# Loading the query weights of a decode step in eight parts of sixteen partitions

## The chip, the cores and the metric

The kernel runs on one core of a Trainium2 chip. The metric is the device time of one execution in microseconds. Before the change it was 380.53 us, the median of three runs (380.45 to 380.88).

The core's engines are TensorE (PE in the profile; its weight loads are PEld), VectorE (DVE), ScalarE (ACT), GpSimd (POOL) and SyncE (SP). Sixteen DMA engines move data between memory and SBUF, the on-chip store of 128 partitions; here SyncE issues all large transfers, ScalarE four small ones.

## The reference

One token passes through an attention block with a cache of 65,536 positions, and through a gated MLP mixer; a gate g mixes the two. All inputs are bfloat16.

```python
# x [1,1,1024]; k_cache, v_cache [1,4,65536,128]; wq [1024,4096]; wo [4096,1024]
q = (x @ wq).reshape(1, 1, 32, 128).transpose(0, 2, 1, 3)
k, v = repeat(k_cache, 8, axis=1), repeat(v_cache, 8, axis=1)
p = softmax(einsum('bhqd,bhkd->bhqk', q, k) * 128 ** -0.5)
a = einsum('bhqk,bhkd->bhqd', p, v).transpose(0, 2, 1, 3).reshape(1, 1, 4096) @ wo

z = gelu(x @ w_in)                       # w_in [1024,3584]
z1, z2 = z[..., :1792], layernorm(z[..., 1792:])
b = (z1 * (w_sp * z2 + b_sp)) @ w_out    # one position: w_sp is one number

g = sigmoid((x * gate_w).sum(-1))
return g * a + (1 - g) * b
```

The caches hold 128 MiB (134 MB) of the 162 MB that the kernel reads.

## The kernel before

**An order written out by hand.** Every operation is recorded by `R.op` (called `P`) with its engine, the keys that it reads and the keys that it writes. A planner derives the semaphore waits from the keys, and each engine runs its operations in the order in which they were recorded. A transfer has a semaphore of its own, named by `dma=`, which counts sixteen when the transfer has landed. A key that was written by a transfer stands for that transfer.

**The stream of loads.** A list `stream` holds all large loads in the order in which they are issued: wq, then K steps 0 and 1 in one load of 8 MB (64 KB for each partition), w_in, K step 2, K step 3, w_out, then K and V in turn, and at the end five loads of wo. They share a ring in SBUF, one row of bytes for each partition. `issue()` sends the next load as soon as the operations that use the bytes under it have been recorded (`done`), and the load then waits on SyncE for these operations. SyncE's queue is in order: a load that waits holds back those behind it.

**The query weights.** wq has 1024 rows of 4096 columns. `rows(A_wq, 0, 8)` gives each of the 128 partitions eight consecutive rows, 65,536 bytes that lie in one piece in memory. `issue()` treats this load in a way of its own (`cut`): the last `MC = 512` columns of the eighth row are left out, so that a partition gets 64,512 bytes, and the missing 128 pieces of 1,024 bytes come through `few_rows()` (L398), right behind the load. That function issues eight small loads into another region of the ring, at `M_AT`: four with five partitions, four apart, of four pieces each, and four with three partitions and four pieces each. Index e of the load numbered `lo` goes to partition 4e + lo.

**Who uses them.** The group of matrix products that ends on L507 computes q. It is recorded as one operation on TensorE (L510), which waits for wq, for the eight small loads, for the transposed input `xT` and for `xe`. Behind it VectorE copies the result (L513), and the load of w_in goes out, since it takes wq's bytes in the ring. Then the K steps begin: VectorE transposes a quarter of a step (L548), TensorE multiplies it, four times for each step. Later, exponentials on ScalarE, V products, and the output products with wo follow; the last ones are at L766, then a copy (L827) and the store (L368).

**The start gate.** A program begins with a barrier between the engines. `emit` takes the first `R.ahead = 2 + MB = 10` instructions of SyncE (the wq load, the eight small loads, and the first K load) and puts them ahead of SyncE's part in this barrier, so that they are issued while the other engines wait for it. In the same way four small loads of ScalarE (`R.early`) go ahead of its part.

## Time and profile before

| what | value |
|---|---|
| median of three runs | 380.53 us |
| the profiled execution | 380.59 us |
| its span, first to last instruction | 379.3 us |
| TensorE busy, share of the span | 229.9 us, 61% |
| VectorE busy | 205.6 us, 54% |
| ScalarE busy | 23.3 us, 6% |
| GpSimd busy | 9.3 us, 2% |
| read from memory | 162.01 MB, 427 GB/s over the span |
| the wq load, 8064 KB, issue to landing | 21.7 us |
| the first K load, 35.4 us from issue, lands at | 42.1 us |
| TensorE begins the products with wq | 23.18 us |

The profile's page lists busy times by engine, the span in forty slices (digits are tenths of a slice; the row GB/s tells what all DMA engines moved in a slice of 9.5 us), the DMA queues, and the groups of instructions. A window's line gives its length, then the busy time and number of instructions for PE, PEld, DVE, ACT and POOL, the granted TensorE clock, the busy share of the DMA engines, and GB/s. In these windows a packet counts wholly where it starts, so the DMA share can be a little over 1. A line of the chain of waits gives the start in us, the length in us, and the line that ran or the transfer that was waited for. A line on a source line's instructions gives minimum, median and maximum of their durations in ns. In the SyncE timeline the columns are start, length, engine, line, and how many instructions.

### The profile page before, as it was taken

To read this page: it belongs to the slowest core of one execution; us is meant where nothing else is said; L and a number is where in the kernel's file an instruction comes from. 1 tells how busy PE (TensorE), PEld (TensorE's weight loads), DVE (VectorE), ACT (ScalarE), POOL (GpSimd) and SP (SyncE) were. 2 spreads that over 40 slices of the span, in tenths; PEclk is the share of its full clock that TensorE was granted. 3 is DMA by queue.
4 is the path that set the end of the run, shared out by engine and by line. 5 is a ranking of instruction groups with operands and counts; after the bars stand their busy time and mean duration, and the time that the engine had idled before them with its cause. 6 is when DMAs were issued, how large, how long until landed. Compare 5 with 4: busy or idle time off the path is not lost.

```text
span 379.3 us, 2599 instructions
## 1 busy us (share of the span) xinstructions
PE 229.9 (61%) x1452; PEld 57.9 (15%) x844; DVE 205.6 (54%) x168; ACT 23.3 (6%) x24; POOL 9.3 (2%) x36
## 2 busy tenths in 40 slices
PE   0062289566648934895389328951995189737296
PEld 0011011011201200121012001220111011201024
DVE  1411487778479625965496249745873387412020
ACT  1000000010420000002200000022000000220000
POOL 1400000000000000000000000000000000000000
PEclk9997589798959985998599959995899589958599
DMA  9999999999999999999999999999999999999896
GB/s 436 435 415 408 433 419 422 442 456 438 408 435 442 435 444 422 422 442 435 442 437 442 429 422 429 444 442 435 429 408 430 442 435 442 437 442 435 384 432 273
DMA packets 3822, 162.17 MB, mean 428 GB/s; under 512 B 484, under 2 KB 612, under 8 KB 868
## 3 DMA queue, kind: packets, MB, share of 16 engines
q1 hardware_dynamic: 3776, 162.01, 98.9%
q8 instruction: 9, 0.15, 0.1%
q10 hardware_dynamic: 36, 0.00, 0.0%
q14 instruction: 1, 0.01, 0.0%
HBM read 162.01 MB, written 0.00 MB: 427 GB/s over the span
## 4 chain that ended last, share of the span: by engine, by line
DMA 61%; PE 17%; DVE 17%; SPq 2%; ACT 1%; issue 1%
DMA arena<-in_A_k_cache_dram 46%; DVE arena L548 16%; DMA arena<-in_A_wo_dram 8%; DMA arena<-in_A_v_cache_dram 7%; PE scp L261 7%; PE scp L263 6%; SPq L409 2%; PE obt L261 2%; PE obt L263 1%; DVE arena L585 1%; PE fbt L766 1%; ACT arena L580 1%; DVE arena L670 0%; DVE arena L668 0%; PE fbt L714 0%
## 5 line engine op out<-in xcount | busy, mean ns | idle before, releaser
L548 DVE STREAM_TRANSPOSE arena<-arena 128x2048 f32<-128x2048 f32 x64 | 143.0, 2284 | 54.9 <-DMA arena<-in_A_k_cache_dram 40.1
L261 PE MATMUL scp<-arena 128*128 128x512 bf16 (+1 forms) x274 | 111.6, 424 | 94.4 <-DVE arena L548 93.9
L263 PE MATMUL scp<-arena 128*128 128x512 bf16 (+1 forms) x275 | 110.2, 418 | 0.0
L261 PE MATMUL obt<-arena 128*64 128x512 bf16 (+2 forms) x334 | 60.7, 404 | 15.1 <-DMA arena<-in_A_v_cache_dram 14.9
L263 PE MATMUL obt<-arena 128*64 128x512 bf16 (+2 forms) x333 | 60.1, 400 | 0.0
L261 PEld LDWEIGHTS scp<-arena 128*128 128x128 bf16 (+1 forms) x274 | 27.5, 104 | 205.1 <-issue 103.9
L585 DVE STREAM_TRANSPOSE arena<-arena 128x2048 bf16<-128x2048 bf16 x7 | 16.2, 2311 | 27.0 <-PE obt L263 24.8
L580 ACT ACTIVATE arena<-arena 128x2048 bf16<-128x2048 f32 x8 | 16.0, 2002 | 217.2 <-DVE arena L577 194.1
L261 PEld LDWEIGHTS obt<-arena 128*64 128x64 bf16 (+1 forms) x334 | 17.7, 109 | 65.3 <-issue 58.5
L565 DVE TENSOR_SCALAR_CACHE_REDUCE arena<-scp 128x2048 f32<-128x2048 f32 x8 | 18.3, 2292 | 16.0 <-PE scp L263 16.0
L614 DVE RECIPROCAL arena<-mbt 128x1 f32<-128x1 f32 x4 | 0.6, 138 | 17.5 <-PE mbt L609 17.5
L588 DVE STREAM_TRANSPOSE arena<-arena 128x1024 bf16<-128x1024 bf16 x2 | 2.5, 1245 | 12.9 <-PE obt L263 12.9
L536 POOL COPY arena<-arena 32x32 bf16<-32x32 bf16 x16 | 3.3, 204 | 227.4 <-PE scp L263 207.7
L467 PE MATMUL scp<-arena 8*128 8x1 bf16 x8 | 0.7, 198 | 13.0 <-DVE arena L462 13.0
L627 PE MATMUL mbt<-arena 128*64 128x128 bf16 x8 | 1.3, 314 | 7.7 <-DVE arena L621 7.7
L766 PE MATMUL fbt<-arena 128*32 128x128 bf16 x128 | 4.2, 220 | 1.2 <-DMA arena<-in_A_wo_dram 1.2
L280 DVE MEMSET mbt<- 128x512 f32 x1 | 0.5, 485 | 7.7 <-PEq L846 7.7
L513 DVE CAST arena<-obt 97x1024 bf16<-97x1024 f32 x1 | 1.2, 1224 | 6.2 <-PE obt L507 6.2
L475 PE MATMUL mbt<-arena 1*128 1x2 bf16 x1 | 0.2, 158 | 7.2 <-DMA arena<-in_B_b_sp_dram 7.2
L827 DVE CAST arena<-fbt 36x128 bf16<-36x128 f32 x1 | 0.3, 283 | 7.3 <-PE fbt L766 7.3
L477 DVE COPY arena<-mbt 128x2 f32<-128x2 f32 x1 | 0.2, 158 | 7.3 <-PE mbt L475 7.3
L577 DVE TENSOR_REDUCE arena<-mbt 128x1 f32<-128x32 f32 x4 | 0.8, 192 | 6.0 <-PE mbt L574 6.0
(99 smaller groups left out, 62.5 us busy)
## 6 DMA issues: line engine op xcount, KB each, us to landing
arena<-in_A_k_cache_dram SPq DMA_DIRECT2D x2, 4096.0 KB, 31.7
arena<-in_A_wq_dram SPq DMA_DIRECT2D x1, 8064.0 KB, 21.7
arena<-in_B_w_in_dram SPq DMA_DIRECT2D x1, 7168.0 KB, 28.9
arena<-in_A_wo_dram SPq DMA_DIRECT2D x1, 4096.0 KB, 38.5
arena<-in_B_w_out_dram SPq DMA_DIRECT2D x1, 3584.0 KB, 20.2
arena<-in_A_wo_dram SPq DMA_DIRECT2D x1, 2048.0 KB, 27.6
arena<-in_A_wo_dram SPq DMA_DIRECT2D x1, 1280.0 KB, 30.3
arena<-in_A_wo_dram SPq DMA_DIRECT2D x1, 512.0 KB, 31.0
```

Source lines behind the costliest of these rows:

```text
L261: return e.matmul(*a, **kw)
L263: one = e.matmul(*a, **kw).ins
L409: P("SP", lambda e, a=a, b=b: e.dma_start(a, b), w=[("few", lo + j0)] + ([] if lo + j0 else [("slot", x) for x in gr]), dma="few%d" % (lo ...
L513: P("DVE", lambda e: e.tensor_copy(psb[0:97, :], ob[0:97, :]), w=["psb", "ob"])
L536: P("POOL", lambda e, pb=pb: e.tensor_copy(vw(qpad, 24 + 32 * pb, [[QP, 4], [1, 8]], 32 * pb, 32), vw(qall, 8 * g, [[32, 4], [1, 8]], 32 * ...
L548: P("DVE", lambda e: e.transpose(ktb(i).bitcast(F32), sl[:, 4096 * p:4096 * (p + 1)].bitcast(F32)), r=keys[4 * p:4 * p + 4], w=[("kt", i % ...
L565: P("DVE", lambda e: e.tensor_scalar(scs(j), scp[:, :], 0.0, None, op0=ALU.add, op1=ALU.max, accum_out=maxc[:, j:j + 1]), w=[("sc", j % 2) ...
L580: P("ACT", lambda e: e.activation(psb2, scs(j), ACTF.Exp, bias=gcol(j // 2, K_NB), scale=SCALE, accum_out=lp[:, j:j + 1]), r=[("sc", j % 2 ...
L585: P("DVE", lambda e: e.transpose(ptsb2, psb2), r=["psb"], w=[("ptsb", 0), ("ptsb", 1)])
L588: P("DVE", lambda e: e.transpose(ptsb(n), ab("PSB", 1024, 1024 * (n % 2))), r=["psb"], w=[("ptsb", n % 2)])
L627: ins = e.matmul(mb[64 * g:64 * (g + 1), 0:128], vw(sel, 128 * c, [[2, 64]]), osc[:, 128 * c:128 * (c + 1)], start=(c == 0), stop=(c == 3) ...
L766: ins = e.matmul(fb[32 * b:32 * (b + 1), 0:QW], ovz[:, z:z + 32], sl[:, o:o + QW], start=False, stop=(i == 3 and c == 7), tile_position=(0 ...
```

## The change

For wq alone, the one load of 128 partitions becomes `NJ = 8` loads of sixteen partitions: load j takes partitions j, j + 8, ..., j + 120, with the same 64,512 bytes for each, from the same place in memory to the same place in SBUF. The first keeps the keys and the semaphore of the old load; each of the other seven writes a key `("wqr", j)` and has a semaphore of its own, and the operation that multiplies with wq reads these keys too. The other loads go the old way. `R.ahead` grows from 10 to 17 instructions, so that the gate stands behind the first K load as before.

```diff
-    MC, MB = 512, 8
+    MC, MB, NJ = 512, 8, 8
...
             cut = keys == [("wq", 0)]
             if cut:
                 w -= MC
-            P("SP", lambda e, o=OFF["RING"] + off, w=w, src=src[:, :w]: e.dma_start(arena[:, o:o + w], src),
-              w=[("slot", x) for x in gr], dma="s%d" % gr[0])
+            o = OFF["RING"] + off
             if cut:
+                for j in range(NJ):
+                    P("SP", lambda e, d=arena[j:128:NJ, o:o + w], src=src[j:128:NJ, :w]: e.dma_start(d, src),
+                      w=[("slot", x) for x in gr] if j == 0 else [("wqr", j)], dma="s%d" % gr[0] if j == 0 else "wqr%d" % j)
                 few_rows()
+            else:
+                P("SP", lambda e, o=o, w=w, src=src[:, :w]: e.dma_start(arena[:, o:o + w], src),
+                  w=[("slot", x) for x in gr], dma="s%d" % gr[0])
             issued[0] += 1
...
-    P("PE", f, r=["xT", "xe"] + keys + [("few", i) for i in range(MB)] + [("slot", x) for x in grains(M_AT, MC * MB)],
+    P("PE", f, r=["xT", "xe"] + keys + [("few", i) for i in range(MB)] + [("wqr", j) for j in range(1, NJ)] + [("slot", x) for x in grains(M_AT, MC * MB)],
       w=["ob"])
...
-    R.ahead = 2 + MB
+    R.ahead = 1 + NJ + MB
```

## The prediction

> **What bounds the kernel now.** I read the page's slices and queue rows first, then the windows, the chain of waits, and last the SyncE timeline.

> ```profile
> span 379.3 us, 2599 instructions
> DMA  9999999999999999999999999999999999999896
> GB/s 436 435 415 408 433 419 422 442 456 438 408 435 442 435 444 422 422 442 435 442 437 442 429 422 429 444 442 435 429 408 430 442 435 442 437 442 435 384 432 273
> q1 hardware_dynamic: 3776, 162.01, 98.9%
> ```

> The queue of SyncE (q1) moves 162.01 MB, and its packets fill 98.9% of sixteen DMA engines for the whole span: 0.989 x 379.3 = 375.1 us. Only 4.2 us of an average DMA engine are free. TensorE with 61% and VectorE with 54% have room. So whatever a DMA engine loses anywhere comes out at the end, one for one, unless it falls into those 4.2 us.

> ```profile
> 0.00:20.70 20.70, 0.83 (x9) 0.66 (x9) 5.46 (x16) 1.28 (x1) 5.99 (x20) 1.00 0.95 402
> 20.70:40.10 19.40, 8.44 (x86) 2.68 (x55) 2.93 (x10) 0.17 (x1) 0.82 (x4) 0.82 1.01 436
> 40.10:345.00 304.90, 199.87 (x1078) 45.80 (x566) 192.11 (x134) 20.78 (x21) 2.45 (x12) 0.83 1.00 435
> 345.00:376.60 31.60, 19.73 (x259) 8.04 (x190) 4.85 (x8) 1.02 (x1) 0.00 (x0) 0.84 0.95 405
> ```

> The last two columns of these windows are the DMA share and GB/s. The rate is flat at 435 to 436 for 320 us, whatever is loaded: 435 / 16 = 27.2 GB/s for each DMA engine. One row of the wq load is 64,512 bytes, so 64,512 / 27.2 = 2.37 us; the trace's own packet records give 2.38 us, nearly the same for every row but an engine's first. Such constancy says that a fixed lane of 27 GB/s is the limit, and not the memory behind it. Two things can be that lane: the DMA engine itself, or the way into a group of SBUF partitions that one DMA engine has to itself in a load of 128. The trace of before can't separate the two, and the change does.

> ```profile
> 0.00 0.40 SPq L392
> 0.45 0.93 SPq L409
> ...
> 6.70 35.40 DMA arena<-in_A_k_cache_dram
> ...
> 345.07 30.26 DMA arena<-in_A_wo_dram
> ```

> The chain starts with SyncE's issues, runs through transfers, and ends on the last of wo; in between it names TensorE and VectorE, but the flat rate shows that transfers run under them.

> **The rows of the changed load.** The load at L392 (128 rows, 8 to each DMA engine) becomes eight loads of 16 rows, partitions j, j+8, ..., j+120. Bytes and row length stay. Sixteen rows over sixteen DMA engines are one row each, so all sixteen write at the same time into partitions that lie 8 apart. No row of the trace shows such a transfer; its cost is bounded so.
> Lower end: the lane is the DMA engine. Each row still takes 2.38 us, eight take 19.0, and the cost is 0.
> Upper end: the lane belongs to a group of partitions. few_rows, right behind the load, is written so that index e has partitions 4e to 4e+3 over four loads; take groups of four as one lane; rows 8 apart then hit every second group, and two DMA engines meet on one lane while another lane stands empty. A row then takes 2 x 2.38 = 4.76 us, eight take 38.1, and the cost is 19.0 us. If the lane serves one of the two first, that one runs ahead and fills the empty lanes; four rows are then late instead of eight: 4 x 2.38 = 9.5 us.
> I take 19.0: the flat rate fits a lane that never gives more than 27.2, the pattern leaves half of such lanes empty, and all DMA engines take their rows in the same order, so neither of a pair gets ahead if the lane alternates.
> [...]

> **The other edits.**
> - Completions: seven more loads mean seven more 4-byte packets per DMA engine, 0.01 us each in the packet records: +0.1 us.
> - Start: the first row of each DMA engine starts at 1.18 to 1.81 us, and the second not 2.38 but on the mean 2.80 us later: 0.42 us of start-up, at most 1.1 (1.18 to 4.67 less 2.38). Two DMA engines on one lane can hide it behind each other: from -1.1 to +1.1 (paid twice), taken -0.4.
> - SyncE issues seven loads more, all ahead of the start gate (L830). Rows that bound one issue:

> ```profile
> L392 SPq DMA_DIRECT2D arena<-in_A_k_cache_dram x9: 327/328/443, 6.7 to 272.1; - x9
> ...
> L392 SPq DMA_DIRECT2D arena<-in_A_wo_dram x5: 328/432/1259, 329.0 to 346.0; - x5
> ...
> 0.45 6.21 SPq L409 DMA_DIRECT2D arena<-in_A_wq_dram  x8
> ```

> At 0.33 us and a gap of 0.04 it is 7 x 0.37 = 2.6 us, at 1.26 us some 9.1. The eight few_rows issues and the first K load are moved back by that; K is issued at 6.70 + 2.6 = 9.3 us (at worst 15.8), while the DMA engines have wq rows until 20.7 even at the old rate. Each issue brings a DMA engine one row of at least 2.38 us, so issuing outruns moving. The cover is 20.7 - 9.3 = 11.4 us; without it all 2.6 us would be idle lanes. The gate too opens 2.6 us later for the other engines (GpSimd, VectorE and ScalarE start at 7.54 to 7.73 now); VectorE's next idle time begins at 14.45 and lasts to 21.7, so 7 us cover it; at the worst 9.1 some 2 us are lost, and fall under the next cover. Cost 0.
> - TensorE waits for seven more semaphores at L507's group (L510), at best 0, by the 0.10 us of a weight load taken as a far bound 0.7 us. Behind it stand VectorE's L513 and, on SyncE, the load of B_w_in, which goes out at 30.14 while K keeps the lanes filled until 40.1: 10 us of cover. Cost 0. If the rows come 19 us later, the K load behind them does too, so this cover moves along.

> **Sum.** The profiled execution took 380.59 us, 379.3 of it span; the median of the runs is 380.53, so the two can stand for each other. 380.6 + 19.0 + 0.1 - 0.4 = **399.3 us**, 4.9% slower. Nothing gives it back later: K, B_w_in and all others follow on the same sixteen lanes, which have 4.2 us of idle time in all, and the first K rows can't start before a DMA engine's eighth wq row is done.

> **Rivals.**
> - *Pairs that drift.* One of two DMA engines is served first: +9.5, with completions 390.2 us. For it: the DMA engines start up to 0.63 us apart. Against it: in before they keep nearly the same distance for all eight rows.
> - *Rows go to the DMA engine that owns the partition*, so the change isn't what it says: no lane is shared, but loads 0 to 3 feed only eight DMA engines, and the others get their first row with the fifth issue, 4 x 0.37 = 1.5 us later. That delay is never recovered by a DMA engine without idle time: 380.6 + 1.5 = 382.1 us.
> - *The lane is the DMA engine.* Nothing but completions and a late issue under cover: 380.7 us. For it: the constant 2.38 us fits it as well. Against it: nothing in the trace.
> - *Faster*: the same, and the first rows come earlier. A single load now hands its sixteen DMA engines their first rows spread over 1.18 to 1.81 us, and start-up goes on to 4.02 to 4.67; if a load of one row each were ready all at once, up to 1.1 us go away. From 380.7, 1.1 less: 379.6 us. It decides if the first rows' delay lies in making the descriptors of eight rows and not in the memory's first answer. Against it: 0.40 us of issuing is little more than the 0.33 of the others, and the DMA engine that starts first also has the longest first row (3.48 us).

> **How the numbers follow.** Shared lane 60% (399.3; own range 396.2 to 401.5: below with start-up at -1.1 and one row of drift, 380.6 + 19.1 - 1.1 - 2.4, above with start-up paid twice and the waits uncovered, 380.6 + 19.1 + 1.1 + 0.7), drift 7%, routed rows 7%, nothing 16%, faster 10%. What a measurement of this kernel can tell from no change is about 0.2%, 0.76 us. Slower: 60 + 7 + 7 = 74%; same 16%; faster 10%. The shared lane alone doesn't make 80%, so the range reaches down over drift, routed rows and no change, 379.9 to 401.5; outside are the faster case and a small rest.

> **What would show it.** Right: the wq loads land near 40 us instead of 21.7; GB/s in the first two slices falls to about half, 220, and is 435 again behind them; the K load lands 19 us later, near 61; from there every stage is the old one, shifted. DMA issues at L409 start near 3 us, the gate opens near 10. Drift: a rate between 220 and 435 until about 40. Wrong: the last wq load lands near 21 to 23 us and the first slices still show over 400. If rows are slow but the end isn't, the claim that no idle time is left falls.

## The result, and the profile after

The changed kernel takes 401.36 us (median of six runs, 401.29 to 401.67) against 380.45 us: a ratio of 1.055, 95% interval 1.0536 to 1.0564, or 20.9 us more. 399.3 us was predicted.

From the page of the changed kernel: span, the row of the DMA engines' busy share, the rate in forty slices of 10 us, and SyncE's queue.

```profile
span 400.1 us, 2610 instructions
DMA  9999999999999999999999999999999999999996
GB/s 207 206 206 206 413 432 427 407 426 439 460 421 439 452 432 414 432 445 426 439 452 421 419 439 445 426 427 445 432 419 441 452 426 426 434 432 419 423 423 279
q1 hardware_dynamic: 3888, 162.01, 98.9%
```

The bytes are the same 162.01 MB, and the DMA engines are as busy as before, 98.9%. But in the first four slices, 40 us, they are busy at half the rate: 206 or 207 GB/s where before had 408 to 436. From the fifth slice on the rate is the old one. A DMA engine counts as busy for as long as a packet takes, so full digits with half the bytes say that each row takes twice as long; they don't say why.

The windows of the changed kernel (last columns: DMA share, GB/s):

```profile
0.00:20.70 20.70, 1.52 (x12) 1.25 (x12) 6.11 (x20) 1.45 (x2) 5.99 (x20) 1.00 0.96 200
20.70:42.00 21.30, 0.00 (x0) 0.00 (x0) 0.53 (x4) 0.00 (x0) 0.00 (x0) 1.00 1.04 227
42.00:62.00 20.00, 9.31 (x83) 2.49 (x52) 1.71 (x3) 0.00 (x0) 0.82 (x4) 0.80 0.99 428
62.00:366.00 304.00, 200.04 (x1078) 45.77 (x566) 192.28 (x134) 20.78 (x21) 2.45 (x12) 0.83 1.00 434
```

The window that holds TensorE's long work (200.04 us of products in 304 us) is the one that before had from 40 to 345 (199.87 us in 304.9), some 21 us later and otherwise unchanged.

SyncE's timeline, and the chain of waits of the first 65 us:

```profile
0.00 5.09 SPq L395 DMA_DIRECT2D arena<-in_A_wq_dram  x8
5.13 6.21 SPq L414 DMA_DIRECT2D arena<-in_A_wq_dram  x8
11.38 0.42 SPq L399 DMA_DIRECT2D arena<-in_A_k_cache_dram  x1
53.12 0.33 SPq L399 DMA_DIRECT2D arena<-in_B_w_in_dram  x1
```

```profile
10.64 33.35 DMA arena<-in_A_wq_dram
43.99 0.88 issue
44.87 0.60 PE obt L261 x4
...
56.21 6.76 another core or an unknown queue
63.00 2.32 DVE arena L553
```

TensorE starts on wq at 44.87 us instead of 23.18, and VectorE gets the first K rows at 63.00 instead of 42.12, 20.9 us later: that is the whole loss, and it stays the same to the end. (The line of 6.76 us is VectorE's wait for the K load; the chain didn't find its transfer.)

The trace's packet records, which lie behind the DMA rows of the views, show the rows themselves: start, length and size of each, though not the DMA engine or the partition. Before, each of the sixteen DMA engines moved its rows of 64,512 bytes in 2.38 us, all but the first. Now the second to fourth and the sixth to eighth take 5.01 to 5.04 us on the mean, the fifth 4.79, and the last row is done at 42.04 us instead of 21.34.

### The profile page after: what moved, and what is told of

Same layout as the page of the kernel before. It is cut to its first block, busy times and chain, and to the rows that moved or that the text cites. A ratio compares the mean times of both kernels' runs of the same rounds, so it can differ in the third digit from the quotient of the medians.

```text
span 400.1 us, 2610 instructions
## 1 busy us (share of the span) xinstructions
PE 231.5 (58%) x1452; PEld 58.2 (15%) x844; DVE 205.6 (51%) x168; ACT 23.3 (6%) x24; POOL 9.3 (2%) x36
## 3 DMA queue, kind: packets, MB, share of 16 engines
q1 hardware_dynamic: 3888, 162.01, 98.9%
HBM read 162.01 MB, written 0.00 MB: 405 GB/s over the span
## 4 chain that ended last, share of the span: by engine, by line
DMA 58%; PE 19%; DVE 17%; SPq 3%; another core or an unknown queue 2%; issue 1%; ACT 1%
DMA arena<-in_A_k_cache_dram 35%; DVE arena L553 15%; DMA arena<-in_A_wq_dram 8%; DMA arena<-in_A_wo_dram 8%; DMA arena<-in_A_v_cache_dram 7%; PE scp L261 7%; PE scp L263 6%; PE obt L261 2%; PE obt L263 2%; SPq L414 1%; SPq L395 1%; DVE arena L590 1%; PE fbt L771 1%; ACT arena L585 1%
## 5 line engine op out<-in xcount | busy, mean ns | idle before, releaser
L261 PE MATMUL obt<-arena 128*64 128x512 bf16 (+2 forms) x334 | 61.5, 413 | 39.4 <-DMA arena<-in_A_wq_dram 24.5
L263 PE MATMUL obt<-arena 128*64 128x512 bf16 (+2 forms) x333 | 60.9, 409 | 0.0
L771 PEld LDWEIGHTS fbt<-arena 128*32 128x32 bf16 x128 | 3.6, 97 | 2.4 <-DMA arena<-in_A_wo_dram 1.2
## 6 DMA issues: line engine op xcount, KB each, us to landing
arena<-in_A_wo_dram SPq DMA_DIRECT2D x1, 4096.0 KB, 38.5
```

The source lines that it names most:

```text
L261: return e.matmul(*a, **kw)
L263: one = e.matmul(*a, **kw).ins
L771: ins = e.matmul(fb[32 * b:32 * (b + 1), 0:QW], ovz[:, z:z + 32], sl[:, o:o + QW], start=False, stop=(i == 3 and c == 7), tile_position=(0 ...
```

## The experiments

The kernels differ from the changed one only in how wq is cut into loads. The lines below, shortened, stand for the destination `arena[j:128:NJ, o:o + w]` and the source `src[j:128:NJ, :w]` of its loop; `NJ`, and with it `R.ahead`, is the number of loads.

The theory under test, "lanes" in the expectations, says: the 128 partitions of SBUF fall into sixteen groups, a group takes in some 27 GB/s whoever writes to it, and DMA engines that write to the same group at the same time share that. The 27 GB/s is a sixteenth of the 435 that the windows of before show; that there are such groups, and that four neighbours and partitions 32 apart are in one, was the author's assumption, and the runs put it to the test. A single time below is one run of that kernel; the kernel before took 380.41 to 380.45 us beside them.

**Eight loads, cut by columns.** Is it the number of loads?

```diff
-  d=arena[j:128:8, o:o + w], src=src[j:128:8, :w]
+  d=arena[:, o + 4032*j:o + 4032*(j + 1)], src=src[:, 4032*j:4032*(j + 1)]
```

> Eight loads as in the changed kernel, but each takes all 128 partitions and an eighth of the columns (8,064 bytes of each row). Theory of lanes (a group of SBUF partitions takes 27 GB/s, and sixteen rows 8 apart reach only half of the groups): each DMA engine writes its own group again, so 380.5 to 381.0 us, and the first two slices of the span are above 400 GB/s. Rival that the number of loads, of issues or of completions is what costs: they are as many as in the changed kernel, so about 401 us and 206 GB/s.

Measured: 380.38 us (ten runs, 380.28 to 380.59), ratio to before 0.9999, interval 0.9989 to 1.0008. Eight issues, their completions, and TensorE's seven more waits cost nothing that shows. SyncE's first lines here:

```profile
0.00 4.01 SPq L397 DMA_DIRECT2D arena<-in_A_wq_dram  x8
4.06 6.20 SPq L416 DMA_DIRECT2D arena<-in_A_wq_dram  x8
10.29 0.42 SPq L401 DMA_DIRECT2D arena<-in_A_k_cache_dram  x1
```

K goes out at 10.29 us instead of 6.70, and the gate opens later in proportion; both are covered. The number of loads is out as a cause. The page's first slice has 361 GB/s and the second 427, so the expected 400 was missed in the first: a packet counts where it starts, and packets of 8 KB reach less far past the end of a slice than those of 64 KB.

**Sixteen partitions, 4 apart.** Is it the distance of 512 KB in memory?

```diff
-  d=arena[j:128:8, ...], src=src[j:128:8, :w]
+  p = slice(64*(j//4) + j%4, 64*(j//4) + 64, 4)
+  d=arena[p, ...], src=src[p, :w]
```

> Eight loads of sixteen partitions, 4 apart instead of 8: four loads in partitions 0 to 63, four in 64 to 127. In memory the sixteen pieces lie 256 KB apart, in the changed kernel 512 KB. Theory of lanes: sixteen partitions 4 apart in one half reach 8 of 16 groups too (32 partitions on is the same group), two DMA engines on each, so 401 us (400 to 402) and 206 GB/s. Rival that the distance in memory costs (512 KB between the DMA engines slow, 256 KB fast): 380.5 to 382 us. Rival that a load with one row for each DMA engine is slow as such: 401 us too, so this run doesn't tell it from the lanes.

Measured: 401.16 us, the first four slices at 207 GB/s. At 256 KB it is as slow as at 512, so 512 KB is nothing special. That no distance matters, this run alone can't say: the runs of sixteen neighbours, of 32 rows (also 256 KB apart, and fast) and of another order in memory do. Nor does it tell the lanes from a fixed price for one row to each DMA engine.

**Sixteen neighbours.**

```diff
+  d=arena[16*j:16*j + 16, ...], src=src[16*j:16*j + 16, :w]
```

> Eight loads of sixteen neighbouring partitions. Theory of lanes: sixteen neighbours reach 4 groups, four DMA engines on each, so a row takes 4 x 2.38 = 9.5 us or, with the loss that pairs showed (5.03 for 4.76), 10.1 us; eight rows 76 to 81 us instead of 19: 437 to 443 us, and about 105 GB/s in the first slices. Rival that a load with one row for each DMA engine is slow as such: 401 us, 206 GB/s. Rival of the distance in memory (64 KB here): no slower than 402 us.

Measured: 434.19 us. From its page:

```profile
GB/s 191 96 95 95 95 167 114 407 460 425 412 436 449 450 424 442 430 438 430 442 430 442 425 430 424 442 430 419 436 436 430 444 424 448 424 450 418 421 422 292
```

The rows took 9.14 us, so sixteen DMA engines moved 16 x 64,512 bytes / 9.14 us = 113 GB/s, about a quarter of 435, as four DMA engines on each of four groups make it. (The slices of 10.8 us show 95 or 191 because a packet counts where it starts, and most of them hold the start of one row for each DMA engine.) A fixed price for a load of one row each (401 us) and the distance in memory (64 KB) are both refuted. The size missed: 9.14 us is less than the 9.5 that was the lower end, and the time is 3 us under the range. 113 GB/s would be 28.2 for each of four groups, more than the 27.1 of one DMA engine alone, so if the theory holds, more than four groups must take in rows at times. By the theory, neighbouring blocks go to two sets of four groups by turns (partitions 0 to 15, then 16 to 31), and the run that follows shows that steps between sets save time (1.1 us for six more), which the range did not allow for. That this is the whole 0.4 us for each row was not tried by itself.

**Turns.** The changed kernel's loads in another order.

```diff
-  for j in range(8)
+  for j in (0, 4, 1, 5, 2, 6, 3, 7)
```

> The eight loads of the changed kernel in the order 0, 4, 1, 5, 2, 6, 3, 7, so that successive loads go to the two halves of the groups in turn. Theory of lanes: where one half follows the other, the earlier of two DMA engines has its new lane to itself until the later one comes, and the later one its old lane; in the changed kernel the one such step (the fifth load) had rows of 4.77 us where the others had 5.03. With seven such steps instead of one: 6 x 0.26 = 1.6 us less, 399.8 us (399 to 400.5). Rivals without lanes: the order doesn't matter, 401.4 us.

Measured: 400.22 us (400.07 to 400.62), ratio to before 1.052, interval 1.0504 to 1.0535, just below that of the changed kernel. Rows from the second on take 4.82 us. Less was saved than expected, 1.1 us and not 1.6, but the time is in the expected range; the rivals without lanes expected no effect of the order.

**Four loads of 32 and two of 64 that reach all groups.** The question is how a load's rows are dealt out.

```diff
+  for j in range(4): d=arena[j:128:4, ...], src=src[j:128:4, :w]   # 32 rows each
+  for j in range(2): d=arena[j:128:2, ...], src=src[j:128:2, :w]   # 64 rows each
```

> Four loads of 32 partitions, 4 apart: each load reaches all 16 groups of SBUF partitions, with two rows for each DMA engine. Theory of lanes, if rows are dealt out in blocks (DMA engine e has rows 2e and 2e + 1 of the load, partitions 8e + j and 8e + 4 + j): in every moment the sixteen again write partitions 8 apart, two on a group, and the halves change with each row: as in the run with turns, 400 us and some 210 GB/s. Theory of lanes, if a load that reaches all groups is dealt out by group: 380.5 to 381 us. Rival that only the number of rows for one DMA engine counts: between, near 390.

> Two loads of 64 partitions, 2 apart, four rows for each DMA engine: each load reaches all 16 groups. Theory of lanes, dealt out in blocks (partitions 8e + j, + 2, + 4, + 6): two on a group, halves change with every second row: 400 to 401.5 us. Dealt out by group: 380.5 to 381 us.

Measured: 380.72 and 380.98 us against 380.45, no more than one run each can tell from no change; rows of 2.38 us, but the first ones 3.15 and 3.11 us where before had 2.79. The windows of the kernel with four loads of 32:

```profile
0.00:20.70 20.70, 1.53 (x12) 1.26 (x12) 6.64 (x23) 1.45 (x2) 5.98 (x20) 1.00 0.96 399
20.70:42.00 21.30, 8.47 (x83) 2.13 (x52) 1.71 (x3) 0.00 (x0) 0.81 (x4) 0.84 1.02 440
```

So a load that reaches all sixteen groups runs at the full rate, 2.38 us for a row, with two or four rows for each DMA engine as with eight. By the theory, dealing out in blocks of neighbouring rows would have put two on a group here too, and so would dealing out in turn (row 0 to the first DMA engine, row 1 to the second, and so on: the first sixteen rows would then reach eight groups). Both are refuted for these shapes. That the rows are dealt out by group is inferred from this; the packet records don't name partitions.

**Two halves of 64 neighbours.**

```diff
+  for j in range(2): d=arena[64*j:64*j + 64, ...], src=src[64*j:64*j + 64, :w]
```

> Two loads of 64 neighbouring partitions, four rows for each DMA engine: each load reaches 8 of 16 groups. Theory of lanes: sixteen DMA engines on 8 groups are two on each, however the rows are dealt out, so 400 to 402 us and 206 GB/s; if the load goes to the eight DMA engines that own these groups alone, no lane is shared, but then the second load must keep the other eight busy: 380.5 to 382. Rival that a load needs several rows for each DMA engine to be fast: 380.5 to 385 us.

Measured: 401.10 us, rows of 5.04 to 5.06 us. From its page:

```profile
GB/s 207 207 207 207 413 439 426 402 426 439 460 421 439 459 426 415 439 439 426 433 459 415 426 420 446 446 428 452 420 426 415 452 452 420 434 433 426 407 431 287
```

The fifth rows, at the step to the other half, took 4.91. With as many rows in a load as the fast run of 64 had, and half the groups, it is as slow as the change. What tells fast from slow is the set of partitions, and not the number of rows.

**Sixteen loads of eight rows, 4 apart.** What does the smallest load cost where nobody shares?

```diff
+  for j in range(16): p = slice(32*(j//4) + j%4, 32*(j//4) + 32, 4)
+                      d=arena[p, ...], src=src[p, :w]
```

> Sixteen loads of eight partitions, 4 apart: 8 rows reach 8 different groups, and only eight DMA engines can take part. Theory of lanes: nobody shares a group, so a row takes 2.38 us although each load is smaller still; eight DMA engines carry sixteen rows each (38 us), the other eight go on to the K load at once. So above 380 GB/s in the first two slices, about half of that in the next two, when the K load of the free eight is done, and the end 8 x 2.38 = 19 us late on the eight that carry more: 399 to 400.5 us. Rival that a load with one row for each DMA engine is slow as such: rows of about 5 us, wq at 80 us, 440 us.

Measured: 418.98 us, neither the 399 to 400.5 of the lanes nor the 440 of the rival. SyncE's timeline and the windows tell why:

```profile
0.00 10.85 SPq L397 DMA_DIRECT2D arena<-in_A_wq_dram  x16
10.90 6.14 SPq L416 DMA_DIRECT2D arena<-in_A_wq_dram  x8
17.07 0.42 SPq L401 DMA_DIRECT2D arena<-in_A_k_cache_dram  x1
```

```profile
1.50:18.70 17.20, 0.00 (x0) 0.00 (x0) 0.48 (x1) 0.81 (x1) 0.50 (x2) 1.00 0.50 210
18.70:22.50 3.80, 0.00 (x0) 0.00 (x0) 3.72 (x12) 0.47 (x1) 3.67 (x11) 1.00 1.38 410
22.50:55.00 32.50, 1.52 (x12) 1.25 (x12) 2.42 (x11) 0.17 (x1) 1.61 (x4) 1.00 0.99 208
```

In the first window eight DMA engines are busy (share 0.50) and move 210 GB/s: 26 GB/s each, and the packet records have their rows at 2.38 us. So loads with one row for each DMA engine aren't slow as such. The K load, though, is issued only at 17.07 us, behind sixteen issues of 0.68 us, gaps included, and the eight small ones, so the other eight DMA engines stand still till then. This step was left out of the expectation. Soon after they start on K, the eight with wq come to their ninth row, the first one in partitions 64 to 127. In the last window all sixteen are busy (0.99) and move no more: 208 GB/s, wq rows at 4.90 us, K rows at 5.00. Loads of the same shape, by the same DMA engines, have rows of 2.38 us alone and of 4.90 beside K rows that belong to another load and lie elsewhere in memory. And it isn't the company of K as such: the eighth wq rows, still in partitions 0 to 63, ran beside the first K rows (from 19.1 us on) in 2.67 to 2.87 us, while the ninth, in partitions 64 to 127, took 4.20 to 4.64. That is the clearest sign for a lane on SBUF's side. It fits the theory if the eight DMA engines with K were writing to partitions 64 to 127 all the while; which partitions they wrote was not shown, as the records name neither partition nor DMA engine.

Nearly the whole loss of 38.5 us lies in these rows: the last wq row ends at 59.5 us instead of 21.3, 38.2 us later.

**The changed partitions, another order in memory.**

```diff
-  d=arena[j:128:8, ...], src=src[j:128:8, :w]
+  d=arena[j:128:8, ...], src=src[16*j:16*j + 16, :w]
```

> The changed kernel's eight loads into partitions 8 apart, but each reads sixteen neighbouring rows of the weights (64 KB apart in memory instead of 512 KB); so the rows of wq lie in other partitions than the products take them for, and q, and with it the output, is not the reference's. The amount of work is the same. Theory of lanes: only the partitions written count: 401.4 us (400.5 to 402), rows of 5.0 us, 206 GB/s. Rival that the distance of 512 KB in memory is slow: 380.5 to 382 us.

Measured: 401.12 us, 207 GB/s in four slices, rows of 5.01 to 5.04 us, the fifth 4.80. The reads are now 64 KB apart and in another order, and nothing changes: the partitions that are written count, and not where in memory the rows lie.

## Why the prediction was right, and where it missed

*What bounds the kernel.* Right. The last wq row of the slowest DMA engine ends 20.7 us later, VectorE gets the first K rows 20.9 later, the span is 20.8 longer, the time 20.9: no step behind it gave anything back, as 4.2 us of idle time in all foretold.

*The rows.* The mechanism was right: of the two lanes that fit a constant 2.38 us, the one on SBUF's side is it (two loads of 64 partitions take 380.98 us when they are 2 apart and 401.10 as neighbours). One step of its working doesn't hold, though. It takes four neighbouring partitions as a lane; that would make 32 lanes, and sixteen rows 8 apart would hit sixteen different ones, with nothing shared and a cost of 0. The runs point to partitions 32 apart sharing a group: eight partitions 4 apart within 32 have rows of 2.38 us, sixteen 4 apart within 64 rows of 5.03, and those take 401.16 us, as long as the sixteen 8 apart (401.36) and a half of 64 neighbours (401.10). So the 19.0 us were right in size for a reason that this step doesn't give. That a row would double was an estimate when 19.0 was taken, and no run had shown it; the runs show rows of 4.99 us on the mean, and 206 GB/s, a little under half of 435.

*The size.* The term that was mis-sized is the doubled row. I took 2 x 2.38 = 4.76 us; rows two to eight took 34.96 us on the mean, 4.99 each, 1.6 us more than 7 x 4.76 = 33.3. The first row, with start-up, came out nearly as taken: the second row starts 2.1 us later on the mean than before, and 2.38 - 0.4 = 1.98 was the sum. So the mean DMA engine is done 20.4 us later (41.37 against 20.98). The rest to 20.7 is spread: the last rows start over 1.36 us instead of 0.66, and the slowest counts. That 401.36 us still lies in the stated range, 0.14 below its end, is luck: the room up there was made for start-up paid twice (+1.1) and waits without cover (+0.7). Neither came, and what filled it, a doubled row of 5.0 instead of 4.76 us, had no term in the range.

*Drift.* It fell: the second rows start spread over 1.35 us and the eighth over 1.36, and rows stay at 5.0 us, so no DMA engine gets ahead. What is real is a small gain where the loads step from one half of the groups to the other: such rows are shorter (4.79 us where the others have 5.01 to 5.04), and seven such steps instead of one gave 1.1 us back in the run with turns.

*Routed rows* fell for loads of sixteen (rows would have stayed at 2.38 us, and took 5.01 to 5.04), and *no change* and *faster* with them. For loads of 32 and 64 rows that reach all groups, dealing out by group is what the runs point to (380.72 and 380.98 us, rows of 2.38).

*The other edits.* Issuing cost more than taken, 0.64 us for each load and not 0.37, so K went out at 11.38 us and not 9.3; it stayed within the cover, as did the gate (VectorE begins at 12.42 us instead of 7.73) and TensorE's waits. The run with eight loads of columns has much the same ones alone (K at 10.29 us), at 380.38 us. The run with eight rows shows the end of the cover: a K load issued at 17.07 us was too late for DMA engines that had no other rows.

## What to carry to other kernels

Where transfers bound a kernel, look at which SBUF partitions are written at the same time, not only at bytes and sizes. Here a load that reaches all sixteen groups of partitions kept the full rate of 2.38 us a row whether it had 32, 64 or 128 rows, and cutting by columns (eight pieces of 8,064 bytes a row) was free (380.38 us against 380.44), while cutting the 128-row load by rows into loads that reach eight or four groups brought 435 GB/s down to 206 or 113. Full DMA digits with half the usual GB/s (9 at 206, where before had 9 at 408 to 436) were the sign. And in this stream, with 4.2 us of idle time in all, the load that was done 20.7 us late at the start made the end 20.9 us later.
